# Decode attention with a GeGLU FFN on one core: longer weight rows in a ring of their own, and attention with the small operands stationary

## The chip, the core and the metric

The kernel runs on one core of a Trainium2 chip. Times are device microseconds (us) of that core; a profiled execution also gives a span, which is about 2 us shorter than the time. Engines: PE (TensorE, with PEld for its weight loads), DVE (VectorE), ACT (ScalarE), POOL (GpSimd), SP (which here only issues DMAs). A matmul loads a *stationary* operand and streams a *moving* one past it; I call one weight load plus one matmul a pair. The granted clock is the share of PE's full clock that the clock records of the profile show; landing records are the times at which each of the 16 DMA engines reports its part of a load as landed. Executions have a fast and a slow state; only fast runs are compared.

## The reference, cut to what matters

```python
xn = layernorm(x)                                   # 8 tokens, D = 512
q  = xn @ wq                                        # 32 heads of 128, 8 KV heads
k, v = last 1024 positions of the caches            # 8 batches x 8 KV heads x 1024 x 128, bf16
s  = (softmax(q @ k.T * Dh**-0.5) @ v) @ wo
g  = silu((gelu(xn @ w_gate) * (xn @ w_up)) @ w_down)   # F = 1792
return x + s * g
```

All of it is read once: 33.6 MB of K and V and 13.9 MB of weights, 47.46 MB by the profile.

## The kernel before

K, V and all weights pass through one ring of 21 slots of 8 KB per partition, in this order: K of group 0, wq, then K and V of 16 groups (4 batches of one KV head each), gate, up, down, wo. The compute loop runs over blocks of 1024 keys: transpose 8 K chunks on PE, copy them to SBUF, use each K^T chunk as the stationary operand for 16 columns of q, take exponentials at the end of a group, and use each V chunk as the stationary operand for 16 columns of P. V runs LAG = 6 blocks behind.

```python
ring = ...tile_pool(name="ring", bufs=21)
s_ps = ps_s.tile([P, P], FP32, name="s_ps")          # accumulator of the output product
nc.vector.memset(s_ps, 0.0)                           # cleared at the start
def score_block(n):
    for c in range(CB):
        nc.tensor.matmul(sc[g][:, s*CB + c, :], kT[n][:, c*P:(c+1)*P], qT_all[:, hkv, b0:b0+I, :], ...)
    if s == NB - 1:                                   # last block of a group: exponentials, ACT
        ...
def value_block(g, s):
    for c in range(s*CB, (s+1)*CB):
        nc.tensor.matmul(oT[g], v_t[g][:, c*Dh:(c+1)*Dh], pT[g][:, c, :], ...)
    if s == NB - 1:                                   # oT[g] is final: times 1/sum, DVE
        ...
# ... after the loop
expand_out(NM - 1); ffn_up(); select_out(NM - 1); ffn_down()
for m in range(NM):                                   # NM = 4 tiles of wo, 32 pairs each
    project_out(m)
# out = x + s_ps * g
```

The softmax here doesn't subtract the row's maximum and nothing guards it: scores larger than these inputs give would overflow.

## Time and profile before

| | before |
|---|---|
| time, median | 123.18 us (123.16 to 123.19) |
| span of the profiled execution | 121.1 us |
| PE / DVE / ACT busy | 71% / 60% / 19% |
| data read from HBM | 47.46 MB, 421 to 428 GB/s in every stage of 10 us from 5 to 105 us |

These lines are from the page of the kernel before: the span, busy time by engine, then slices of a fortieth of the span (DMA is the busy share of the 16 DMA engines in tenths), the main DMA queue, and the chain of work that ended last.

```profile
span 121.1 us, 4123 instructions
...
PE 86.0 (71%) x1856; PEld 71.1 (59%) x1856; DVE 72.3 (60%) x150; ACT 22.6 (19%) x70; POOL 2.4 (2%) x15
...
DMA  3999999999999999999999999999999999999820
GB/s 84 387 430 430 430 427 417 419 430 425 425 427 427 425 414 422 430 419 430 425 427 422 422 417 430 422 425 422 425 433 418 422 414 434 416 430 423 341 88 5
...
q1 hardware_dynamic: 6800, 47.46, 93.7%
...
DMA 82%; PE 12%; DVE 2%; SPq 1%; issue 0%
```

The DMA engines are full from the second slice to the thirty-seventh, and 82% of the chain is DMA: in the body the kernel is as fast as its loads. The next lines are from the timeline of the kernel before (start, duration, engine, line, operation, count, and in brackets the idle time ahead of the first instruction and what ended it).

```profile
93.11 0.61 PE L282 MATMUL kT_ps<-ident,slot 128*128 128x128 bf16 x8
...
95.28 1.14 ACT L304 ACTIVATE pT<-sc_ps,diag 128x128 bf16<-128x128 f32 x4 [2.39 <-PE sc_ps L294]
...
96.85 1.05 PE L329 MATMUL m_ps<-pT,slot 128*128 128x16 bf16 x32
...
98.70 7.69 PE L402 MATMUL m_ps<-slot,xpT_sb 128*32 128x512 bf16 x32
...
108.52 1.12 PE L437 MATMUL m_ps<-slot,hT_sb 128*8 128x128 bf16 x56 [0.55 <-DVE m_ps L433]
...
109.96 1.02 PE L383 MATMUL s_ps<-slot,oE_1066 128*8 128x128 bf16 x32 [0.32 <-DMA slot<-in_A_wo_dram]
...
112.40 1.02 PE L383 MATMUL s_ps<-slot,oE_1569 128*8 128x128 bf16 x32 [1.42 <-DMA slot<-in_A_wo_dram]
...
114.84 1.02 PE L383 MATMUL s_ps<-slot,oE_2072 128*8 128x128 bf16 x32 [1.42 <-DMA slot<-in_A_wo_dram]
...
116.75 1.02 PE L383 MATMUL s_ps<-slot,oE_2360 128*8 128x128 bf16 x32 [0.88 <-DMA slot<-in_A_wo_dram]
```

The four tiles of the output product each wait for their weights, and the kernel ends 1.02 us of PE work (plus two DVE steps and the store) after the last large piece lands.

### The profile page before, as it was taken

How to read it: one execution, taken by the hardware profiler on the slowest of the kernel's cores; microseconds unless marked ns; L12 is line 12 of the kernel's file. 1: busy time of each engine (PE TensorE's matmuls, PEld its weight loads, DVE VectorE, ACT ScalarE, POOL GpSimd, SP SyncE). 2: the span in 40 equal slices, each digit the busy share in tenths (PEclk: the TensorE clock that was granted, in tenths of full speed). 3: DMA queues.
4: the chain of work that ended last, by engine and by line, in shares of the span. 5: the costliest groups of instructions: out<-in, count | busy, mean ns of one | idle time of the engine just before them, and what ended most of it. 6: DMA issues, size and time to landing. Idle time of an engine off the chain costs nothing.

```text
span 121.1 us, 4123 instructions
## 1 busy us (share of the span) xinstructions
PE 86.0 (71%) x1856; PEld 71.1 (59%) x1856; DVE 72.3 (60%) x150; ACT 22.6 (19%) x70; POOL 2.4 (2%) x15
## 2 busy tenths in 40 slices
PE   0075269696875968999997969566798789955450
PEld 0061029586865957999896969565698542134340
DVE  2352046866956749678989987747798670562000
ACT  0440000321303301212330330303033300300000
POOL 6100000000000000000000000000000000000000
PEclk9999756999999985559999999999999756995555
DMA  3999999999999999999999999999999999999820
GB/s 84 387 430 430 430 427 417 419 430 425 425 427 427 425 414 422 430 419 430 425 427 422 422 417 430 422 425 422 425 433 418 422 414 434 416 430 423 341 88 5
DMA packets 6929, 47.73 MB, mean 394 GB/s; under 512 B 888, under 2 KB 896, under 8 KB 1920
## 3 DMA queue, kind: packets, MB, share of 16 engines
q1 hardware_dynamic: 6800, 47.46, 93.7%
q8 instruction: 14, 0.23, 0.7%
q10 hardware_dynamic: 112, 0.02, 0.1%
q14 instruction: 3, 0.02, 0.1%
HBM read 47.46 MB, written 0.01 MB: 392 GB/s over the span
## 4 chain that ended last, share of the span: by engine, by line
DMA 82%; PE 12%; DVE 2%; SPq 1%; issue 0%
DMA slot<-in_A_k_cache_dram 44%; DMA slot<-in_B_w_gate_dram 16%; DMA slot<-in_A_wo_dram 15%; DMA slot<-in_A_wq_dram 7%; PE kT_ps L282 7%; PE m_ps L329 2%; PE sc_ps L294 2%; SPq L91 1%; PE s_ps L383 1%; DVE kT L286 1%; PE m_ps L316 1%; DVE sums L318 1%; SPq L103 0%; PE m_ps L370 0%; DVE tmp L483 0%
## 5 line engine op out<-in xcount | busy, mean ns | idle before, releaser
L286 DVE COPY kT<-kT_ps 128x1024 bf16<-128x1024 bf16 x64 | 42.2, 677 | 18.1 <-PE kT_ps L282 17.5
L282 PE MATMUL kT_ps<-ident,slot 128*128 128x128 bf16 x512 | 43.4, 234 | 9.9 <-DMA slot<-in_A_k_cache_dram 9.5
L282 PEld LDWEIGHTS <-slot 128*128 128x128 bf16 x512 | 32.6, 104 | 13.3 <-DMA slot<-in_A_k_cache_dram 10.1
L304 ACT ACTIVATE pT<-sc_ps,diag 128x128 bf16<-128x128 f32 x64 | 18.2, 368 | 70.6 <-PE sc_ps L294 70.6
L294 PE MATMUL sc_ps<-qT_all,kT 128*128 128x16 bf16 x512 | 22.9, 171 | 0.3 <-issue 0.3
L329 PE MATMUL m_ps<-pT,slot 128*128 128x16 bf16 x512 | 21.8, 170 | 1.2 <-issue 1.1
L329 PEld LDWEIGHTS <-slot 128*128 128x128 bf16 x512 | 18.6, 97 | 4.6 <-issue 3.1
L294 PEld LDWEIGHTS <-kT 128*128 128x128 bf16 x512 | 20.4, 99 | 0.0
L318 DVE TENSOR_REDUCE sums<-m_ps 128x16 f32<-128x512 f32 x16 | 10.9, 684 | 1.2 <-PE m_ps L316 1.2
L402 PE MATMUL m_ps<-slot,xpT_sb 128*32 128x512 bf16 x32 | 7.7, 1105 | 0.0
L316 PE MATMUL m_ps<-pT,ones_pp 128*128 128x512 bf16 x16 | 6.7, 416 | 0.7 <-ACT pT L304 0.7
L250 PE MATMUL m_ps<-slot,xnT_sb 128*32 128x512 bf16 x32 | 3.5, 527 | 4.2 <-DMA slot<-in_A_wq_dram 4.2
L234 PE MATMUL m_ps<-ident,xhat 8*128 8x8 bf16 x4 | 0.3, 168 | 7.0 <-DVE xhat L214 7.0
L259 DVE CAST q_sb<-m_ps 128x512 bf16<-128x512 f32 x2 | 1.3, 686 | 6.6 <-PE m_ps L250 6.6
L356 DVE TENSOR_TENSOR wide<-m_ps,hmask 64x1024 bf16<-64x1024 bf16 x4 | 4.9, 1216 | 0.5 <-PE m_ps L352 0.4
L483 DVE TENSOR_TENSOR tmp<-s_ps,g_sb 128x128 f32<-128x128 f32 x1 | 0.3, 292 | 7.1 <-PE s_ps L383 7.1
L250 PEld LDWEIGHTS <-xnT_sb 128*32 128x32 bf16 x32 | 0.8, 101 | 6.2 <-issue 5.8
L322 DVE RECIPROCAL recip<-sums 128x16 f32<-128x16 f32 x16 | 4.0, 253 | 0.6
L234 PEld LDWEIGHTS <-xhat 8*128 8x128 bf16 x4 | 0.2, 102 | 7.0 <-DVE xhat L214 7.0
L402 PEld LDWEIGHTS <-xpT_sb 128*32 128x32 bf16 x32 | 1.7, 117 | 4.3 <-issue 3.4
L338 DVE TENSOR_TENSOR oT_all<-m_ps,recip 128x16 bf16<-128x16 f32 x16 | 3.5, 218 | 0.4 <-PE m_ps L329 0.3
L352 PE MATMUL m_ps<-ident,oT_all 128*64 128x128 bf16 x4 | 1.0, 253 | 2.7 <-DVE sums L318 2.1
(71 smaller groups left out, 33.4 us busy)
## 6 DMA issues: line engine op xcount, KB each, us to landing
slot<-in_A_k_cache_dram SPq DMA_DIRECT2D x16, 1024.0 KB, 19.4
slot<-in_A_v_cache_dram SPq DMA_DIRECT2D x16, 1024.0 KB, 19.7
slot<-in_A_wq_dram SPq DMA_DIRECT2D x4, 1024.0 KB, 8.6
slot<-in_A_wo_dram SPq DMA_DIRECT2D x3, 1024.0 KB, 18.0
slot<-in_B_w_gate_dram SPq DMA_DIRECT2D x2, 896.0 KB, 20.0
slot<-in_B_w_up_dram SPq DMA_DIRECT2D x2, 896.0 KB, 18.9
slot<-in_B_w_down_dram SPq DMA_DIRECT2D x2, 896.0 KB
slot<-in_A_wo_dram SPq DMA_DIRECT2D x1, 768.0 KB, 17.7
```

What stands on the lines that cost most here:

```text
L250: nc.tensor.matmul(q_ps[n][Q * q : Q * (q + 1), :], xnT_sb[:, k, :], wq_t[k][:, hkv * NW : (hkv + 1) * NW], start=(k == 0), stop=(k == NDC ...
L282: nc.tensor.transpose(t_ps[:, c * P : (c + 1) * P], k_t[g][:, cc * Dh : (cc + 1) * Dh], ident)
L286: nc.vector.tensor_copy(out=kT[n], in_=t_ps)
L294: nc.tensor.matmul(sc[g][:, s * CB + c, :], kT[n][:, c * P : (c + 1) * P], qT_all[:, hkv, b0 : b0 + I, :], start=True, stop=True,)
L304: nc.scalar.activation(out=pT[g][:, :, i * rep : (i + 1) * rep], in_=sc[g][:, :, i * rep : (i + 1) * rep], func=ACT.Exp, bias=diag[:, i : ...
L316: nc.tensor.matmul(sums_ps, ones_pp, pT[g], start=True, stop=True)
L318: nc.vector.tensor_reduce(out=sums, in_=sums_ps.rearrange("p c m -> p m c"), axis=AX.X, op=ALU.add)
L322: nc.vector.reciprocal(out=recip[g], in_=sums)
L329: nc.tensor.matmul(oT[g], v_t[g][:, c * Dh : (c + 1) * Dh], pT[g][:, c, :], start=(c == 0), stop=(c == C - 1),)
L338: nc.vector.tensor_tensor(out=oT_all[:, hkv * rep : (hkv + 1) * rep, b0 : b0 + I].rearrange("p j i -> p i j"), in0=oT[g].rearrange("p (i j ...
L356: nc.vector.tensor_tensor(out=wide, in0=t_ps.rearrange("p (q e) -> p e q", e=HS) .unsqueeze(2) .to_broadcast([HS * B, HS, HS, DQ]), in1=hm ...
L402: nc.tensor.matmul(gu_ps[w][Q * q : Q * (q + 1), :], xpT_sb[:, k, :], cols[:, j0[q] : j0[q] + JQ, :], start=(k == 0), stop=(k == NDC - 1), ...
```

## The change

Its intent: fewer, longer DMA rows for the weights, and far fewer PE instructions in attention. (1) Weights go through a ring of 4 slots of 16 KB; the K/V ring shrinks to 11. (2) q becomes the stationary operand, padded with zeros to 32 columns so that two groups share a tile, and K^T is the moving one, in four column tiles. (3) Exponentials are taken for a head (two groups) at a time; DVE transposes P in 32x32 blocks. (4) P is the stationary operand for V, in four column tiles whose partial sums a closing fp32 product with a selection matrix adds up. (5) To find PSUM banks, the output accumulator moves into a pool of the loop and is cleared at its first use. Not shown in the cut below: 16 of the 64 copies of K^T move from DVE to ACT, and the smaller pools get fewer buffers.

```diff
-    ring = ctx.enter_context(tc.tile_pool(name="ring", bufs=21))
+    ring = ctx.enter_context(tc.tile_pool(name="ring", bufs=11))
+    wide_ring = ctx.enter_context(tc.tile_pool(name="wide_ring", bufs=4))
 ...
+    def score_half(g, a):
+        for kb in range(P // Q):
+            nc.tensor.matmul(sc[hkv][Q * kb : Q * (kb + 1), a],
+                qz[:, hkv, half].rearrange("p h m -> p (h m)"),
+                kT[2 * g + a][:, :, Q * kb : Q * (kb + 1)], ...)
+    def exp_head(hkv): ...                  # ACT, 4 x 256 columns
+    def turn_head(hkv): nc.vector.transpose(out=pT[hkv]..., in_=p_sb[hkv]...)
 ...
     def value_block(g, s):
+            nc.tensor.matmul(o_ps[g][Q * t : Q * (t + 1), :],
+                pT[hkv][:, half, 2 * y : 2 * y + 2, :].rearrange("p c m -> p (c m)"),
+                v_t[g][:, 2 * y * Dh : (2 * y + 2) * Dh], ...)
+            o_sb[g] = small.tile([P, 2, Dh], FP32, name="o_sb")
+            nc.scalar.copy(out=o_sb[g]..., in_=o_ps[g])
+    def close_group(g):
+        for c in range(2):
+            nc.tensor.matmul(fin, o_sb[g][:, c, :], pick[:, c, :], start=(c == 0), stop=(c == 1))
 ...
     def project_out(m):
+        if m == 0:
+            s_ps.append(ps_o.tile([P, P], FP32, name="o_ps"))
+            nc.vector.memset(s_ps[0], 0.0)
 ...
-    LA, LAG = 2, 6
+    LA, LAG = 2, 13
 ...
+    for part in range(2):
+        expand_out(NM - 1, part)
     ffn_up()
     select_out(NM - 1)
     ffn_down()
     ...
     for m in range(NM):                     # NM is now 2, 64 pairs each
         project_out(m)
```

More of the change, by code (lines that the diff above doesn't have):

```diff
@@ L53 @@
     SLOT = C * Dh
+    WSLOT = 2 * SLOT
     JF = F // P
@@ L62 @@
     front.tile([P, 96], FP32, name="front_pad")
-    ring = ctx.enter_context(tc.tile_pool(name="ring", bufs=21))
+    ring = ctx.enter_context(tc.tile_pool(name="ring", bufs=11))
+    wide_ring = ctx.enter_context(tc.tile_pool(name="wide_ring", bufs=4))
     consts = ctx.enter_context(tc.tile_pool(name="consts", bufs=1))
     persist = ctx.enter_context(tc.tile_pool(name="persist", bufs=1))
-    kT_pool = ctx.enter_context(tc.tile_pool(name="kT_pool", bufs=4))
-    p_pool = ctx.enter_context(tc.tile_pool(name="p_pool", bufs=3))
-    small = ctx.enter_context(tc.tile_pool(name="small", bufs=3))
+    kT_pool = ctx.enter_context(tc.tile_pool(name="kT_pool", bufs=3))
+    p_pool = ctx.enter_context(tc.tile_pool(name="p_pool", bufs=2))
+    small = ctx.enter_context(tc.tile_pool(name="small", bufs=2))
     ps_kT = ctx.enter_context(tc.tile_pool(name="ps_kT", bufs=3, space=bass.MemoryType.PSUM))
-    ps_sc = ctx.enter_context(tc.tile_pool(name="ps_sc", bufs=2, space=bass.MemoryType.PSUM))
-    ps_m = ctx.enter_context(tc.tile_pool(name="ps_m", bufs=2, space=bass.MemoryType.PSUM))
-    ps_s = ctx.enter_context(tc.tile_pool(name="ps_s", bufs=1, space=bass.MemoryType.PSUM))
+    ps_sc = ctx.enter_context(tc.tile_pool(name="ps_sc", bufs=1, space=bass.MemoryType.PSUM))
+    ps_o = ctx.enter_context(tc.tile_pool(name="ps_o", bufs=2, space=bass.MemoryType.PSUM))
+    ps_m = ctx.enter_context(tc.tile_pool(name="ps_m", bufs=1, space=bass.MemoryType.PSUM))
     ctx.enter_context(tc.manual_schedule())
@@ L82, in slot, with wide_slot @@
         return ring.tile([P, SLOT], BF16, name="slot")
+    def wide_slot():
+        return wide_ring.tile([P, WSLOT], BF16, name="wide_slot")
     k_t, v_t, wo_t = {}, {}, {}
-    wq_t, wg_t, wu_t, wd_t = [], [], [], []
+    wq_t, ffn_t = [], []
     def load_cache(src, g):
@@ L100, in load_wq @@
     def load_wq():
-        for k in range(NDC):
-            t = slot()
-            nc.sync.dma_start(out=t, in_=A_wq[k * P : (k + 1) * P, :])
-            wq_t.append(t)
-    def load_ffn():
-        for dst, src in ((wg_t, B_w_gate), (wu_t, B_w_up)):
-            for a in range(2):
-                t = slot()
-                nc.sync.dma_start(
-                    out=t[:, 0 : 2 * F],
-                    in_=src[a * 2 * P : (a + 1) * 2 * P, :].rearrange(
-                        "(p k) f -> p (k f)", k=2
-                    ),
-                )
-                dst.append(t[:, 0 : 2 * F].rearrange("p (k f) -> p k f", k=2))
-        JH = JF // 2
-        wd = B_w_down.rearrange("(p j) d -> p j d", j=JF)
-        for a in range(2):
-            t = slot()[:, 0 : JH * D].rearrange("p (j d) -> p j d", j=JH)
-            nc.sync.dma_start(out=t, in_=wd[:, a * JH : (a + 1) * JH, :])
-            wd_t.extend(t[:, j, :] for j in range(JH))
-    HS = SLOT // D
+        for a in range(2):
+            t = wide_slot()
+            src = A_wq[a * 2 * P : (a + 1) * 2 * P, :].rearrange("(p k) n -> p (k n)", k=2)
+            nc.sync.dma_start(out=t, in_=src)
+            t = t.rearrange("p (k n) -> p k n", k=2)
+            wq_t.extend(t[:, k, :] for k in range(2))
+    def load_ffn():
+        for src, k in ((B_w_gate, NDC), (B_w_up, NDC), (B_w_down, JF)):
+            n = src.shape[0] * src.shape[1] // P
+            t = wide_slot()[:, 0:n]
+            nc.sync.dma_start(out=t, in_=src.rearrange("(p k) f -> p (k f)", k=k))
+            ffn_t.append(t.rearrange("p (k f) -> p k f", k=k))
+    HS = WSLOT // D
     NM = Hq // HS
@@ L129, in load_wo @@
     def load_wo(m, cut=HS):
-        t = slot().rearrange("p (e d) -> p e d", e=HS)
+        t = wide_slot().rearrange("p (e d) -> p e d", e=HS)
         src = A_wo[m * HS * Dh : (m + 1) * HS * Dh, :].rearrange("(p e) d -> p e d", e=HS)
@@ L157 @@
     nc.vector.memset(eps_sb, 1e-5)
-    sel = consts.tile([P, R, I], FP32, name="sel")
+    sel = consts.tile([P, P // IR, I, rep], FP32, name="sel")
     nc.gpsimd.memset(sel, 0.0)
@@ L162 @@
         out=sel, in_=sel, compare_op=ALU.not_equal, fill=1.0, base=0,
-        pattern=[[-I, R], [-1, I]], channel_multiplier=1,
+        pattern=[[-IR, P // IR], [-rep, I], [-1, rep]], channel_multiplier=1,
     )
@@ L166 @@
     nc.vector.tensor_reduce(
-        out=diag, in_=sel.rearrange("p r i -> p i r"), axis=AX.X, op=ALU.add
+        out=diag, in_=sel.rearrange("p k i j -> p i k j"), axis=AX.XY, op=ALU.add
     )
@@ L171 @@
     )
+    pick = consts.tile([P, 2, IR], FP32, name="pick")
+    nc.gpsimd.memset(pick, 0.0)
+    for t in range(P // Q):
+        nc.gpsimd.affine_select(
+            out=pick, in_=pick, compare_op=ALU.not_equal, fill=1.0, base=-Q * t,
+            pattern=[[-IR, 2], [-1, IR]], channel_multiplier=1,
+        )
     hmask = consts.tile([HS * B, HS], BF16, name="hmask")
@@ L222 @@
     nc.gpsimd.memset(xpT_sb, 0.0)
-    qT_all = persist.tile([P, Hkv, B, rep], BF16, name="qT_all")
+    qz = persist.tile([P, Hkv, GPH, GPH, IR], BF16, name="qz")
+    nc.gpsimd.memset(qz, 0.0)
     oT_all = persist.tile([P, Hq, B], BF16, name="oT_all")
@@ L226 @@
     g_sb = persist.tile([P, P], FP32, name="g_sb")
-    s_ps = ps_s.tile([P, P], FP32, name="s_ps")
-    nc.vector.memset(s_ps, 0.0)
     def transpose_x():
         t = ps_m.tile([P, 2, NDC, B], BF16, name="m_ps")
+        xn = xhat.rearrange("b (a p k) -> b a k p", a=2, k=2)
+        xp = xhat.rearrange("b (p k) -> b k p", k=NDC)
         for k in range(NDC):
-            nc.tensor.transpose(t[:, 0, k, :], xhat[:, k * P : (k + 1) * P], ident[0:B, 0:B])
-        xp = xhat.rearrange("b (a p k) -> b a k p", a=2, k=2)
-        for a in range(2):
-            for k in range(2):
-                nc.tensor.transpose(t[:, 1, 2 * a + k, :], xp[:, a, k, :], ident[0:B, 0:B])
+            nc.tensor.transpose(t[:, 0, k, :], xn[:, k // 2, k % 2, :], ident[0:B, 0:B])
+        for k in range(NDC):
+            nc.tensor.transpose(t[:, 1, k, :], xp[:, k, :], ident[0:B, 0:B])
         nc.vector.tensor_copy(out=xnT_sb[:, :, 0:B], in_=t[:, 0])
@@ L245, in project_q @@
         q_sb = persist.tile([P, Hkv // NQ, NW], BF16, name="q_sb")
-        q_ps = [ps_m.tile([P, NW], FP32, name="m_ps") for n in range(Hkv // NQ)]
+        q_ps = [ps_o.tile([P, NW], FP32, name="o_ps") for n in range(Hkv // NQ)]
         for k in range(NDC):
@@ L268, in project_q @@
         for n in range(Hkv // NQ):
-            nc.vector.tensor_copy(
-                out=qT_all[:, n * NQ : (n + 1) * NQ],
-                in_=t_ps[:, n, :, :, 0:B].rearrange("p j q b -> p q b j"),
-            )
-    kT, sc, pT, oT = {}, {}, {}, {}
+            for a in range(GPH):
+                nc.vector.tensor_copy(
+                    out=qz[:, n * NQ : (n + 1) * NQ, a, a, :].rearrange(
+                        "p q (b j) -> p q b j", b=I
+                    ),
+                    in_=t_ps[:, n, :, :, a * I : (a + 1) * I].rearrange("p j q b -> p q b j"),
+                )
@@ L277, in transpose_block @@
+    kT, sc, pT, p_sb, o_ps, o_sb, recip = {}, {}, {}, {}, {}, {}, {}
     def transpose_block(n):
         g, s = n // NB, n % NB
-        t_ps = ps_kT.tile([P, CB * P], BF16, name="kT_ps")
+        t_ps = ps_kT.tile([P, CB, P], BF16, name="kT_ps")
         for c in range(CB):
             cc = s * CB + c
-            nc.tensor.transpose(
-                t_ps[:, c * P : (c + 1) * P], k_t[g][:, cc * Dh : (cc + 1) * Dh], ident
-            )
-        kT[n] = kT_pool.tile([P, CB * P], BF16, name="kT")
@@ L286, in transpose_block @@
-        nc.vector.tensor_copy(out=kT[n], in_=t_ps)
-    def score_block(n):
-        g, s = n // NB, n % NB
-        hkv, b0 = g // GPH, (g % GPH) * I
+            nc.tensor.transpose(t_ps[:, c, :], k_t[g][:, cc * Dh : (cc + 1) * Dh], ident)
+        if n % 2 == 0:
+            kT[n // 2] = kT_pool.tile([P, 2 * CB, P], BF16, name="kT")
+        dst = kT[n // 2][:, (n % 2) * CB : (n % 2 + 1) * CB, :]
+        if n % (2 * NB) in (3, 6):
+            nc.scalar.copy(out=dst, in_=t_ps)
+        else:
+            nc.vector.tensor_copy(out=dst, in_=t_ps)
@@ new lines, in score_half @@
+    def score_half(g, a):
+        hkv, half = g // GPH, g % GPH
+        if half == 0 and a == 0:
+            sc[hkv] = ps_sc.tile([P, 2, 2 * CB, Q], FP32, name="sc_ps")
+        for kb in range(P // Q):
+            nc.tensor.matmul(
+                sc[hkv][Q * kb : Q * (kb + 1), a],
+                qz[:, hkv, half].rearrange("p h m -> p (h m)"),
+                kT[2 * g + a][:, :, Q * kb : Q * (kb + 1)],
+                start=(half == 0),
+                stop=(half == GPH - 1),
+                skip_group_check=True,
+            )
@@ new lines, in exp_head, with turn_head @@
+    def exp_head(hkv):
+        p_sb[hkv] = p_pool.tile([P, C * Q], BF16, name="p_sb")
+        src = sc[hkv].rearrange("p a c (r i) -> p (a c r) i", i=I)
+        dst = p_sb[hkv].rearrange("p (n i) -> p n i", i=I)
+        for i in range(I):
+            nc.scalar.activation(
+                out=dst[:, :, i], in_=src[:, :, i], func=ACT.Exp,
+                bias=diag[:, i : i + 1], scale=inv_sqrt_dh,
+            )
+    def turn_head(hkv):
+        pT[hkv] = p_pool.tile([P, GPH, C, IR], BF16, name="pT")
+        nc.vector.transpose(
+            out=pT[hkv].rearrange("p h c m -> p c h m"),
+            in_=p_sb[hkv].rearrange("p (c h m) -> p c h m", c=C, h=GPH),
+        )
@@ new lines, in sum_head @@
+    def sum_head(hkv):
+        sums_ps = ps_m.tile([P, GPH, CB, IR], FP32, name="m_ps")
+        for s in range(NB):
+            nc.tensor.matmul(
+                sums_ps, ones_pp, pT[hkv][:, :, s * CB : (s + 1) * CB, :],
+                start=(s == 0), stop=(s == NB - 1),
+            )
+        sums = small.tile([P, GPH, IR], FP32, name="sums")
+        nc.vector.tensor_reduce(
+            out=sums, in_=sums_ps.rearrange("p h c m -> p h m c"), axis=AX.X, op=ALU.add
+        )
+        recip[hkv] = small.tile([P, GPH, IR], FP32, name="recip")
+        nc.vector.reciprocal(out=recip[hkv], in_=sums)
@@ L291, in score_block, with value_block @@
+    def value_block(g, s):
+        hkv, half = g // GPH, g % GPH
         if s == 0:
-            sc[g] = ps_sc.tile([P, C, IR], FP32, name="sc_ps")
-        for c in range(CB):
+            o_ps[g] = ps_o.tile([P, 2 * Dh], FP32, name="o_ps")
+        for y in range(s * CB // 2, (s + 1) * CB // 2):
+            t = y % (P // Q)
             nc.tensor.matmul(
-                sc[g][:, s * CB + c, :],
-                kT[n][:, c * P : (c + 1) * P],
-                qT_all[:, hkv, b0 : b0 + I, :],
-                start=True,
-                stop=True,
+                o_ps[g][Q * t : Q * (t + 1), :],
+                pT[hkv][:, half, 2 * y : 2 * y + 2, :].rearrange("p c m -> p (c m)"),
+                v_t[g][:, 2 * y * Dh : (2 * y + 2) * Dh],
+                start=(y < P // Q),
+                stop=(y >= C // 2 - P // Q),
+                skip_group_check=True,
@@ L300, in score_block @@
             )
         if s == NB - 1:
-            pT[g] = p_pool.tile([P, C, IR], BF16, name="pT")
-            for i in range(I):
-                nc.scalar.activation(
-                    out=pT[g][:, :, i * rep : (i + 1) * rep],
-                    in_=sc[g][:, :, i * rep : (i + 1) * rep],
-                    func=ACT.Exp,
-                    bias=diag[:, i : i + 1],
-                    scale=inv_sqrt_dh,
-                )
-    recip = {}
-    def sum_group(g):
-        sums_ps = ps_m.tile([P, C, IR], FP32, name="m_ps")
-        nc.tensor.matmul(sums_ps, ones_pp, pT[g], start=True, stop=True)
-        sums = small.tile([P, IR], FP32, name="sums")
-        nc.vector.tensor_reduce(
-            out=sums, in_=sums_ps.rearrange("p c m -> p m c"), axis=AX.X, op=ALU.add
-        )
-        recip[g] = small.tile([P, IR], FP32, name="recip")
-        nc.vector.reciprocal(out=recip[g], in_=sums)
@@ L324, in value_block @@
-    def value_block(g, s):
-        if s == 0:
-            sum_group(g)
-            oT[g] = ps_m.tile([P, IR], FP32, name="m_ps")
-        for c in range(s * CB, (s + 1) * CB):
-            nc.tensor.matmul(
-                oT[g],
-                v_t[g][:, c * Dh : (c + 1) * Dh],
-                pT[g][:, c, :],
-                start=(c == 0),
-                stop=(c == C - 1),
-            )
-        if s == NB - 1:
-            hkv, b0 = g // GPH, (g % GPH) * I
-            nc.vector.tensor_tensor(
-                out=oT_all[:, hkv * rep : (hkv + 1) * rep, b0 : b0 + I].rearrange(
-                    "p j i -> p i j"
-                ),
-                in0=oT[g].rearrange("p (i j) -> p i j", i=I),
-                in1=recip[g].rearrange("p (i j) -> p i j", i=I),
-                op=ALU.mult,
-            )
@@ L347 @@
-    oE, wide_t = {}, {}
-    def expand_out(m):
-        t_ps = ps_m.tile([HS * B, Dh], BF16, name="m_ps")
-        nc.tensor.transpose(
-            t_ps, oT_all[:, m * HS : (m + 1) * HS, :].rearrange("p h b -> p (h b)"), ident
-        )
-        wide = small.tile([HS * B, HS, HS, DQ], BF16, name="wide")
-        nc.vector.tensor_tensor(
-            out=wide,
-            in0=t_ps.rearrange("p (q e) -> p e q", e=HS)
-            .unsqueeze(2)
-            .to_broadcast([HS * B, HS, HS, DQ]),
-            in1=hmask.unsqueeze(1).unsqueeze(3).to_broadcast([HS * B, HS, HS, DQ]),
+            o_sb[g] = small.tile([P, 2, Dh], FP32, name="o_sb")
@@ new lines, in value_block @@
+            nc.scalar.copy(out=o_sb[g].rearrange("p c d -> p (c d)"), in_=o_ps[g])
+    def close_group(g):
+        hkv, half = g // GPH, g % GPH
+        fin = ps_m.tile([P, IR], FP32, name="m_ps")
+        for c in range(2):
+            nc.tensor.matmul(fin, o_sb[g][:, c, :], pick[:, c, :], start=(c == 0), stop=(c == 1))
+        nc.vector.tensor_tensor(
+            out=oT_all[:, hkv * rep : (hkv + 1) * rep, half * I : (half + 1) * I].rearrange(
+                "p j i -> p i j"
+            ),
+            in0=fin.rearrange("p (i j) -> p i j", i=I),
+            in1=recip[hkv][:, half, :].rearrange("p (i j) -> p i j", i=I),
@@ L362, in expand_out @@
             op=ALU.mult,
         )
-        wide_t[m] = wide
+    oE, wide_t, x_ps, s_ps = {}, {}, {}, []
+    def expand_out(m, part):
+        if part == 0:
+            x_ps[m] = ps_m.tile([HS * B, Dh], BF16, name="m_ps")
+            nc.tensor.transpose(
+                x_ps[m], oT_all[:, m * HS : (m + 1) * HS, :].rearrange("p h b -> p (h b)"), ident
+            )
+            wide_t[m] = small.tile([HS * B, HS, HS, DQ], BF16, name="wide", bufs=1)
+        HE = HS // 2
+        es = slice(part * HE, (part + 1) * HE)
+        nc.vector.tensor_tensor(
+            out=wide_t[m][:, es],
+            in0=x_ps[m].rearrange("p (q e) -> p e q", e=HS)[:, es]
+            .unsqueeze(2)
+            .to_broadcast([HS * B, HE, HS, DQ]),
+            in1=hmask.unsqueeze(1).unsqueeze(3).to_broadcast([HS * B, HE, HS, DQ]),
+            op=ALU.mult,
+        )
@@ L383, in project_out @@
                 nc.tensor.matmul(
-                    s_ps[32 * q : 32 * q + B, :],
+                    s_ps[0][32 * q : 32 * q + B, :],
                     oE[m][:, e, :],
@@ L396, in ffn_up @@
     def ffn_up():
-        gu_ps = [ps_m.tile([P, JQ * P], FP32, name="m_ps") for w in range(2)]
-        for w, wt in enumerate((wg_t, wu_t)):
+        gu_ps = [ps_o.tile([P, JQ * P], FP32, name="o_ps") for w in range(2)]
+        for w, wt in enumerate(ffn_t[0:2]):
             for k in range(NDC):
-                cols = wt[k // 2][:, k % 2, :].rearrange("x (p j) -> x j p", j=JF)
+                cols = wt[:, k, :].rearrange("x (p j) -> x j p", j=JF)
                 for q in range(NQ):
@@ L439, in ffn_down @@
                     hT_sb[:, j - j0[r], Q * r : Q * r + B],
-                    wd_t[j][:, q * P : (q + 1) * P],
+                    ffn_t[2][:, j, q * P : (q + 1) * P],
                     start=(j == 0),
@@ L450, in ffn_down @@
         nc.vector.tensor_tensor(out=g_sb, in0=th2, in1=f_ps, op=ALU.mult)
-    LA, LAG = 2, 6
+    LA, LAG = 2, 13
     N = NG * NB
+    NH = GPH * NB
     transpose_x()
-    for n in range(LA):
+    for n in range(NB):
         transpose_block(n)
     project_q()
-    for n in range(N + LAG):
-        if n + LA < N:
-            transpose_block(n + LA)
-        if n < N:
-            score_block(n)
-        if n >= LAG:
-            g, s = (n - LAG) // NB, (n - LAG) % NB
-            value_block(g, s)
-            GM = HS // rep * GPH
-            if g % GM == 0 and g > 0:
-                if s == 0:
-                    expand_out(g // GM - 1)
-                if s == 3:
-                    select_out(g // GM - 1)
-    expand_out(NM - 1)
+    for n in range(LA, N + LAG + NB):
+        if NB <= n < N:
+            transpose_block(n)
+        k = n - LA
+        if 0 <= k < N and k % 2 == 1:
+            score_half(k // NB, k % NB // 2)
+            if k % NH == NH - 1:
+                exp_head(k // NH)
+        if n >= NH and n % NH == 3 and n // NH <= Hkv:
+            turn_head(n // NH - 1)
+        if n >= NH and n % NH == 4 and n // NH <= Hkv:
+            sum_head(n // NH - 1)
+        v = n - LAG
+        if 0 <= v < N:
+            value_block(v // NB, v % NB)
+        if v >= NB and v % NB == 1:
+            g = v // NB - 1
+            close_group(g)
+        if v == N // 2 + 2:
+            expand_out(0, 0)
+        if v == N // 2 + 4:
+            expand_out(0, 1)
+        if v == N // 2 + 6:
+            select_out(0)
+    for part in range(2):
+        expand_out(NM - 1, part)
     ffn_up()
@@ L482 @@
     tmp = small.tile([P, P], FP32, name="tmp")
-    nc.vector.tensor_tensor(out=tmp, in0=s_ps, in1=g_sb, op=ALU.mult)
+    nc.vector.tensor_tensor(out=tmp, in0=s_ps[0], in1=g_sb, op=ALU.mult)
     out_sb = small.tile([P, P], BF16, name="out_sb")
```

## The prediction

> **What bounds it now.** The DMA stream. The table of stages shows 418 to 434 GB/s and full engines from 5 to 112 us; the queue table has 47.46 MB on one queue. In the chain of waits DMA is 82%, PE 12%. PE (71% busy), DVE (60%) and ACT (19%) wait: by the list of waits PE waits 9.5 us and its weight loads 10.1 us for K tiles.
>
> In the packet records rows of 8192 B take 309 ns, 7168 B 272 ns, 2048 B 84 ns: about 27.7 B/ns plus 12 to 13 ns per row.
>
> The engines do not finish together. By the landing records, the last load reaches them between 114.2 and 117.3 us. The lag grows in steps of about 1.4 us, each after one of the 14 16-KB instruction fetches (22.5 to 113.7 us). The first eight hit eight different engines; from the ninth (76.3 us) the same ones are hit again, so the last engine is 3.1 us behind. They follow PE's 3712 instructions, one per 256.
>
> Tail: the last 0.75 MB lands at 116.7 us, then 32 matmul and weight-load pairs of project_out take 1.02 us, then two DVE steps and the store, to 121.1 us.
>
> **What the change does.**
> 1. Weight rows: 1920 become 1024 (q 512→256, FFN 768→384, out 640→384). 896 × 12.5 ns / 16 engines = −0.7 us. The Trainium skill, "DMA: Bandwidth & Descriptors" (Why small descriptors are slow), says each packet has a fixed overhead; this trace agrees, with its 12 ns.
> 2. PE pairs fall from 1856 to about 1246 (scores 512→128, V 512→256, +32 closing): 2492 instructions, so 9 fetches instead of 14. With 8 the last engine would be hit once (−1.5 us). The ninth falls near instruction 2304, as project_out begins (111 to 113 us), and probably still delays an already hit engine. I expect −0.2 us at 70%, −1.5 us at 30%.
> 3. Tail: after the last tile's large piece lands, 64 pairs are left instead of 32: +1.0 us.
> 4. P turned on DVE, extra copies on ACT, fp32 closing matmuls: off the critical path (DVE near 65 us, ACT near 45 us).
> 5. The ring shrinks from 21 to 11 slots and V is consumed 13 blocks after K instead of 6. An estimate from traced durations (a block's transposes 0.46 us at full clock, 0.9 at half) leaves 10 us of slack before a V slot is needed again, less 2 to 3 us of PE lag: no DMA gap at full clock. At half clock for long, it would stall. The last output tile waits for the gate's slot, free at about 104 us, needed at about 109 us.
>
> Sum: −0.7 −0.5 +1.0, plus a small allowance for stalls;
>
> **Predicted: 122.8 us, 80% range 121.3 to 124.6. Faster by over 2%: 0.08; within 2%: 0.80; slower by over 2%: 0.12.**
>
> **What would show it.** Right: 16 KB rows near 605 ns; 420 GB/s or more in all loop stages; 9 instruction fetches; 64 pairs of about 2 us after the last large landing; PE well below 71% at nearly the same time. Wrong: stages under 410 GB/s with DMA issues waiting for PE (ring too small) or for the gate's matmuls.
>
> **What would make it wrong.** A clock that stays at half, since more of PE is transposes: PE lags over 7 us and the ring starves (125 us or more). Only eight effective fetches, or a cheaper tail: 121.5 us or less.

## The result, and the profile after

The changed kernel takes **127.49 us** (127.23 to 127.53), against 123.18 us. The ratio is 1.0346 with a 95% interval of 1.0328 to 1.0364. (A ratio is the mean time of one kernel's fast runs over that of the other's of the same rounds, so not quite the ratio of the medians quoted.) The prediction, 122.8 us with a range to 124.6, was wrong.

The same page lines after the change:

```profile
span 125.8 us, 3010 instructions
...
PE 94.7 (75%) x1294; PEld 60.8 (48%) x1294; DVE 66.5 (53%) x126; ACT 45.8 (36%) x70; POOL 4.1 (3%) x21
...
DMA  3999999999999999999999999999999999988000
GB/s 86 417 449 423 404 427 435 417 425 427 435 419 422 427 430 417 425 427 425 422 435 414 427 425 425 427 425 422 444 436 425 433 421 438 354 292 344 0 5 3
...
q1 hardware_dynamic: 5792, 47.45, 90.2%
...
PE 38%; DMA 36%; DVE 11%; ACT 8%; issue 3%; SPq 1%; DVEq 0%; ACTq 0%
```

Up to slice 34 (107 us) the DMA rows look like those of before: the loop did not starve. Then the rate dips (354, 292, 344) and the last three slices, over 9 us, move nothing, where before only the last slices were thin. The chain has turned over: DMA went from 82% to 36%, and PE, DVE and ACT together from 14% to 57%. So the loads are not what the end waits for. The timeline of the changed kernel shows what is, from the last K transposes on:

```profile
92.16 0.61 PE L290 MATMUL kT_ps<-ident,slot 128*128 128x128 bf16 x8
...
94.01 2.53 ACT L320 ACTIVATE p_sb<-sc_ps,diag 128x256 bf16<-128x256 f32 x4 [0.21 <-PE sc_ps L306]
...
96.56 1.25 DVE L327 STREAM_TRANSPOSE pT<-p_sb 128x1024 bf16<-128x1024 bf16 x1 [1.58 <-ACT p_sb L320]
...
97.87 0.61 PE L335 MATMUL m_ps<-pT,ones_pp 128*128 128x256 bf16 x4 [2.92 <-DVE pT L327]
...
99.34 1.04 PE L369 MATMUL m_ps<-pick,o_sb 128*128 128x16 f32 x4
...
101.45 1.03 PE L369 MATMUL m_ps<-pick,o_sb 128*128 128x16 f32 x4
...
103.57 1.03 PE L369 MATMUL m_ps<-pick,o_sb 128*128 128x16 f32 x4 [0.53 <-ACT o_sb L363]
...
105.14 7.47 PE L439 MATMUL o_ps<-wide_slot,xpT_sb 128*32 128x512 bf16 x32
...
115.67 1.66 PE L474 MATMUL m_ps<-wide_slot,hT_sb 128*8 128x128 bf16 x56 [0.65 <-DVE m_ps L470]
...
118.48 0.17 DVE L417 MEMSET o_ps<- 128x128 f32 x1
118.70 3.59 PE L420 MATMUL o_ps<-wide_slot,oE 128*8 128x128 bf16 x128 [1.36 <-DVE o_ps L417]
```

Read it against the timeline before. The last K block is transposed 0.95 us *earlier* (92.77 against 93.72 us), but the FFN's first product starts at 105.14 instead of 98.70 us. Between them everything runs in series: exponentials of a whole head, the turn on DVE, sums, V, and three closings of about a microsecond each, with an ACT copy ahead of each. Then the output product starts only after the accumulator is cleared at 118.48 us, which DVE does behind the gate's last step, and all 128 pairs are still to do when they start at 118.70 us, 1.9 us after the last weights have landed (116.8 us by the landing records).

The account in microseconds closes:

| | before | after | difference |
|---|---|---|---|
| last K block transposed to FFN start (the drain) | 4.98 | 12.37 | +7.39 |
| last K block transposed, when | 93.72 | 92.77 | -0.95 |
| FFN start until output pairs could start, without DMA waits | 10.95 | 13.56 | +2.61 |
| all output pairs | 4.08 | 3.59 | -0.49 |
| sum of these | | | +8.56 |
| slack that before had | | | -4.04 |
| **end of the output product, 117.77 to 122.29** | | | **+4.52** |

The change's chain is 8.6 us longer; the first 4 us vanished in the slack; the rest is the 4.3 us of the result (4.5 in these two profiled executions).

Two more views. First, engine busy time and clock by stage; the columns are the stage, its length, busy us (instructions) of PE, PEld, DVE, ACT and POOL, then PE's granted clock, the DMA share and GB/s. After the change:

```profile
85.00:95.00 10.00, 8.73 (x128) 5.62 (x120) 5.97 (x11) 6.13 (x10) 0.00 (x0) 1.00 1.02 432
95.00:105.00 10.00, 6.07 (x53) 4.06 (x53) 2.71 (x6) 2.65 (x6) 0.00 (x0) 0.67 1.02 432
105.00:115.00 10.00, 8.53 (x53) 1.66 (x53) 5.70 (x8) 1.23 (x2) 0.00 (x0) 0.82 0.91 358
```

PE stood idle for 2.92 us waiting for the turn (to 97.87 us), and by the clock records the granted clock fell from 1.00 to 0.50 at 98.45 us: in the rest of the drain PE works at half speed. (The kernel before loses clock here too, at 95.51 us, although PE was idle for no longer than 0.40 us at a stretch in the 3.4 us ahead of it, so the length of an idle stretch alone does not explain when the clock falls. But its drain is 5 us long, not 12.) Second, the waits of the DMA queue's own sequencer, after the change (who waited for whom, total us, times, longest):

```profile
SPq L96 <- PE kT_ps L290: 28.3, 17, 2.3
SPq L132 <- DMA wide_slot<-in_B_w_gate_dram: 13.9, 1, 13.9
...
SPq L132 <- PE o_ps L439: 11.5, 1, 11.5
```

The small ring does make loads wait for PE (28.3 us in total), but with loads queued 18 us ahead this opened no gap. The last line is a real gap: the second half of wo needs the gate's slot, which is free only when the late FFN has read it, at 109.0 us. That is the dip in the GB/s row, and it is a rival explanation of the loss.

### The profile page after: what moved, and what is told of

It is laid out like the page before. It is cut to its first block, busy times and chain, and to the rows that moved or that the text cites. A ratio compares the mean times of both kernels' runs of the same rounds, so it can differ in the third digit from the quotient of the medians.

```text
span 125.8 us, 3010 instructions
## 1 busy us (share of the span) xinstructions
PE 94.7 (75%) x1294; PEld 60.8 (48%) x1294; DVE 66.5 (53%) x126; ACT 45.8 (36%) x70; POOL 4.1 (3%) x21
## 4 chain that ended last, share of the span: by engine, by line
PE 38%; DMA 36%; DVE 11%; ACT 8%; issue 3%; SPq 1%; DVEq 0%; ACTq 0%
DMA slot<-in_A_k_cache_dram 29%; PE kT_ps L290 13%; DMA wide_slot<-in_A_wq_dram 7%; ACT p_sb L320 6%; PE m_ps L369 5%; PE o_ps L353 5%; PE sc_ps L306 4%; DVE pT L327 4%; PE o_ps L439 3%; PE o_ps L420 3%; PE m_ps L335 3%; SPq L96 1%; PE m_ps L474 1%; DVE kT L297 1%; DVE wide L391 1%
## 5 line engine op out<-in xcount | busy, mean ns | idle before, releaser
L290 PEld LDWEIGHTS <-slot 128*128 128x128 bf16 x512 | 33.7, 107 | 12.8 <-issue 5.8
L297 DVE COPY kT<-kT_ps 128x1024 bf16<-128x1024 bf16 x48 | 32.9, 688 | 12.4 <-PE kT_ps L290 12.3
L295 ACT COPY kT<-kT_ps 128x1024 bf16<-128x1024 bf16 x16 | 16.7, 1046 | 25.2 <-PE kT_ps L290 21.4
L320 ACT ACTIVATE p_sb<-sc_ps,diag 128x256 bf16<-128x256 f32 x32 | 20.3, 826 | 3.7 <-PE sc_ps L306 3.7
L353 PE MATMUL o_ps<-slot,pT 128*32 128x256 bf16 x256 | 18.3, 300 | 0.0
L306 PE MATMUL sc_ps<-kT,qz 128*32 128x512 bf16 x128 | 13.4, 409 | 6.0 <-ACT p_sb L320 5.4
L327 DVE STREAM_TRANSPOSE pT<-p_sb 128x1024 bf16<-128x1024 bf16 x8 | 10.0, 1244 | 7.5 <-ACT p_sb L320 7.5
L369 PE MATMUL m_ps<-pick,o_sb 128*128 128x16 f32 x64 | 11.1, 288 | 1.9 <-DVE wide L391 1.1
L369 PEld LDWEIGHTS m_ps<-pick,o_sb 128*128 128x128 f32 x64 | 9.6, 214 | 5.0 <-ACT o_sb L363 2.2
L439 PE MATMUL o_ps<-wide_slot,xpT_sb 128*32 128x512 bf16 x32 | 7.5, 1090 | 0.0
```

Of the source, the lines that this page charges most:

```text
L290: nc.tensor.transpose(t_ps[:, c, :], k_t[g][:, cc * Dh : (cc + 1) * Dh], ident)
L295: nc.scalar.copy(out=dst, in_=t_ps)
L297: nc.vector.tensor_copy(out=dst, in_=t_ps)
L306: nc.tensor.matmul(sc[hkv][Q * kb : Q * (kb + 1), a], qz[:, hkv, half].rearrange("p h m -> p (h m)"), kT[2 * g + a][:, :, Q * kb : Q * (kb ...
L320: nc.scalar.activation(out=dst[:, :, i], in_=src[:, :, i], func=ACT.Exp, bias=diag[:, i : i + 1], scale=inv_sqrt_dh,)
L327: nc.vector.transpose(out=pT[hkv].rearrange("p h c m -> p c h m"), in_=p_sb[hkv].rearrange("p (c h m) -> p c h m", c=C, h=GPH),)
```

## The experiments

Theory T: the loss is the serial tail (drain, FFN, late clearing, all 128 pairs). Rival R1: the load that waits for the gate's slot. Rival R2: the small ring or the long rows. All kernels gave correct results. "Before" on the chips of these runs was 123.14 to 123.15 us; the changed kernel was not run again beside them, so gains are against its 127.49 us.

### Halves of the change: `x4_weights_only`, `x5_attention_only`

```diff
  # x4: before.py with load_wq, load_ffn, load_wo, ring 11 + wide ring 4 of the change; attention of before
  # x5: the change with load_wq, load_ffn, load_wo of before, one ring of 20 slots; attention of the change
```

> The attention of before with the long weight rows, their ring of 4 and the small ring of 11 slots. Theory T: -0.7 us for 896 fewer rows, +1.0 us for 64 pairs instead of 32 after the last large piece, perhaps 0.5 us for the wait for the gate's buffer: 123.0 to 124.2 us. Rival R2 (ring or rows are the loss): 126 us or more.

> The new attention with the weight slots of before (20 slots of 8 KB rows, no wide ring). Theory T: the drain stays, FFN starts near 105 us and the 128 output pairs start near 118.5 us, with all weights already landed: 126.5 to 127.7 us. Rival R2: near 123.2 us. Rival R1: near 123.2 us as well, since no load waits for the gate.

Weights only: 123.51 us (123.43 to 123.63), ratio 1.0028 [1.0010, 1.0046]. Attention only: 126.59 us (126.20 to 127.25), ratio 1.0284 [1.0242, 1.0325]. Each as T expected. R2 falls: with the small ring and the long rows the time is +0.4 us. R1 falls as the main cause: in the second kernel no load waits for the gate's matmuls, all weights have landed by 115.7 us, and the end is as late. These are its FFN and output product:

```profile
105.43 7.47 PE L446 MATMUL o_ps<-slot,xpT_sb 128*32 128x512 bf16 x32
...
118.30 3.59 PE L427 MATMUL o_ps<-slot,oE 128*8 128x128 bf16 x128 [1.36 <-DVE o_ps L424]
```

The first kernel ends as the kernel before does, with a wait for its last weights:

```profile
116.42 1.88 PE L380 MATMUL s_ps<-wide_slot,oE 128*8 128x128 bf16 x64 [2.36 <-DMA wide_slot<-in_A_wo_dram]
```

### The wait for the gate's slot alone: `x2_gate_own`

```diff
+        for a in range(2):                       # gate into two slots of the K/V ring
+            t = slot()[:, 0 : 2 * F].rearrange("p (k f) -> p k f", k=2)
+            nc.sync.dma_start(out=t, in_=B_w_gate.rearrange("(p k) f -> p k f", k=NDC)[:, 2*a : 2*a + 2, :])
-        for src, k in ((B_w_gate, NDC), (B_w_up, NDC), (B_w_down, JF)):
+        for src, k in ((B_w_up, NDC), (B_w_down, JF)):
```

> The gate weights go into two of the small slots, so the last output load no longer waits for the gate's matmuls. Theory T: the DMA gap at 110 to 115 us closes and the last load lands near 115 us, but the output pairs still start at about 118.7 us, so 127.2 to 127.7 us, no change. Rival R1: the time falls by 2 to 4 us.

Two of its four runs were slow (up to 129.03 us), which makes the median 128.19; the two fast ones are 126.84 and 127.49 us, ratio 1.0325 [1.0287, 1.0362]. (The slow two are slow by their time; their granted clocks, 0.906 and 0.891, are not lower than those of the fast two, and why they are slow stays open.) The gap closed (last load landed at 115.4 instead of 116.8 us) and the output pairs still waited for the clearing:

```profile
117.95 3.59 PE L428 MATMUL o_ps<-wide_slot,oE 128*8 128x128 bf16 x128 [1.36 <-DVE o_ps L425]
```

A DMA gap in full view of the GB/s row cost nothing that the two fast runs show (0.65 us apart), because something else was later.

### The accumulator: `x1_acc_early`

```diff
     def project_out(m):
-        if m == 0:
-            s_ps.append(ps_o.tile([P, P], FP32, name="o_ps"))
-            nc.vector.memset(s_ps[0], 0.0)
 ...
+        if n == N + 1:                            # in a bank that the K transposes have left
+            s_ps.append(ps_kT.tile([P, P], FP32, name="kT_ps"))
+            nc.vector.memset(s_ps[0], 0.0)
```

> Theory T (the loss is the serial drain: last exponentials, turn, values, fp32 closing, then FFN, then all 128 output pairs): the output pairs waited 1.36 us for the accumulator's clearing, which VectorE does only after the gate; with the accumulator cleared before the tail the pairs start right behind the down projection, so 126.1 us (-1.2 to -1.4 against the changed kernel's 127.5). Rival R1 (the last output load waits for the gate's buffer, and that load is the limit): it lands at about 116.5 us in any case, so less than 0.5 us is gained. Rival R2 (small ring or weight rows): no change.

125.24 us (125.07 to 126.35), ratio 1.0187 [1.0141, 1.0234]: 2.2 us gained, more than the wait itself. Its trace says why:

```profile
115.87 1.67 PE L471 MATMUL m_ps<-wide_slot,hT_sb 128*8 128x128 bf16 x56 [0.65 <-DVE m_ps L467]
...
117.32 2.58 PE L417 MATMUL kT_ps<-wide_slot,oE 128*8 128x128 bf16 x128
```

The pairs now follow the down projection without a pause, and they take 2.58 us instead of 3.59: the granted clock was back at 1.00 from 118.6 us, where the changed kernel still had 0.50. That the missing pause of 1.36 us brought this raise is argued, not shown: in y1b (next section) the clock rose at 118.95 us, with the same pause still there. The run at 126.35 us perhaps missed that raise; it was not profiled.

### The closing product: `y1_close_bf16`, `y1b_close_bf16`

```diff
-    pick = consts.tile([P, 2, IR], FP32, name="pick")
+    pick = consts.tile([P, 2, IR], BF16, name="pick")
-            o_sb[g] = small.tile([P, 2, Dh], FP32, name="o_sb")
+            o_sb[g] = small.tile([P, 2, Dh], BF16, name="o_sb")
```

> The closing product in bf16 instead of fp32 (32 pairs instead of 64, each cheaper). Theory T: the three closings behind the last K tile took 1.04, 1.03 and 1.03 us at half clock and lie in the serial drain, so FFN starts 1.5 to 2 us earlier (103.2 instead of 105.1 us) and the time is 125.5 to 126.2 us. A rival in which the end is set by DMA or by FFN's own weights gives no change from 127.5.

> The bf16 closing once more, because its profile fell into a slow execution and its fast runs gained 3.1 us where I had expected 1.5 to 2. If the gain is real it comes again (124.0 to 124.8 us), and its trace shows where: FFN should start at 102 to 103 us instead of 105.1, the rest a clock that is back at full speed in the tail or K tiles finished earlier in the loop.

The three fast executions of the first run took 123.71 to 124.43 us, ratio 1.0082 [1.0052, 1.0111] (its median, 124.37 us, includes a slow one); the second run took 124.32 us (124.29 to 124.66), ratio 1.0094 [1.0077, 1.0111]: two lines return 3.2 of the 4.3 us. I had expected 1.5 to 2. The last closing and the FFN in the second run's trace:

```profile
101.63 0.22 PE L369 MATMUL m_ps<-pick,o_sb 128*128 128x16 bf16 x2 [0.54 <-ACT o_sb L363]
...
102.40 7.56 PE L439 MATMUL o_ps<-wide_slot,xpT_sb 128*32 128x512 bf16 x32
```

A closing fell from 1.03 to 0.22 us at the same low clock, and it is 2 pairs instead of 4. FFN starts 2.74 us earlier: 2.0 us from the three closings, 0.75 us because the loop, where 13 more of them stand, is shorter too. Most of the rest is the output pairs (3.35 instead of 3.59 us).

One execution of the first run took 144.88 us (slow, not compared), and the profile fell on it. Eight K transposes took 0.94 to 1.07 us in it, instead of 0.61 us. The kernel before takes 1.01 to 1.04 us for them where its clock is 0.52 (45 to 55 us), so PE ran at about half speed in this execution, though its page has no clock row at all (the table of stages prints 1.00 where there are no records). The reason for that state stays open. The DMA rate fell to 277 GB/s in the loop, and the queue waited 26.2 us for the gate's slot. This is the failure that the prediction named under "what would make it wrong"; it is not what the ordinary runs do.

### The clock in the drain: `y4_keep_warm`

```diff
+        if n == N + 4:                            # while PE waits for the last turn
+            t = ps_kT.tile([P, 4, P], FP32, name="kT_ps")
+            for _ in range(13):
+                nc.tensor.matmul(t, ones_pp, kT[N // 2 - 1][:, 0:4, :], start=True, stop=True)
```

> The changed kernel plus 13 dummy products of 512 columns on PE in the 3 us in which it waits for the last head's exponentials and turn (result unchanged). If the fallen clock (0.5 from about 97.8 us) is a part of the drain's cost, the drain from the turn to FFN shrinks from 7.3 us to 5 to 6 us and the time falls by 1 to 2.5 us; if the drain is latency of the hops between engines alone, it stays within 0.5 us of 127.5.

125.41 us (124.92 to 126.39), ratio 1.0191 [1.0133, 1.0249]: 2.1 us gained by useless work. Stages of this run (columns as above):

```profile
95.00:98.00 3.00, 2.84 (x16) 1.19 (x13) 1.41 (x2) 1.75 (x4) 0.00 (x0) 1.00 0.96 402
98.00:101.00 3.00, 2.34 (x38) 1.46 (x37) 1.03 (x4) 0.75 (x2) 0.00 (x0) 1.00 1.02 435
```

The second of these stages in the changed kernel:

```profile
98.00:101.00 3.00, 2.90 (x36) 1.87 (x34) 1.01 (x3) 0.37 (x1) 0.00 (x0) 0.57 0.97 416
```

And a closing, from the timeline of y4 again:

```profile
100.93 0.62 PE L369 MATMUL m_ps<-pick,o_sb 128*128 128x16 f32 x4 [0.32 <-ACT o_sb L363]
```

The clock stays at 1.00 through the drain (it falls at 104.19 us, in the FFN), where the changed kernel had 0.57 from 98 to 101 us, and an fp32 closing takes 0.62 us. So about 1.6 us of the drain (FFN at 103.52 instead of 105.14 us) is the fallen clock. The gains of this section overlap: a cheaper closing is worth less when the clock is up.

### Both small edits: `u1_bf16_acc_early`

The edits are those of y1b and x1 together, on the changed kernel.

> Bf16 closing and early accumulator together, everything else as changed. Both shorten the same serial tail, so they add: the accumulator's 1.4 us of waiting on top of 124.4, 122.6 to 123.6 us; if the clock's part of both gains is the same microsecond, 123.5 or above. If they did not lie on the same chain, the smaller one would vanish.

123.40 us (123.33 to 123.57), ratio 1.0023 [1.0008, 1.0038]. Two small edits, none in the stream or the loop's structure, return 4.1 of the 4.3 us. Alone they returned 2.2 and 3.2; the sum is smaller, since the clock's part of x1's gain is missing here: in u1's trace the output pairs take 3.9 us (114.17 to 118.06 us, with a pause of 0.42 us that the profile puts to no wait) instead of 2.58:

```profile
114.17 3.01 PE L417 MATMUL kT_ps<-wide_slot,oE 128*8 128x128 bf16 x109
...
117.61 0.45 PE L417 MATMUL kT_ps<-wide_slot,oE 128*8 128x128 bf16 x19 [0.42 <-issue]
```

### A tail in another order: `y2_ffn_first`, `y3_ffn_first_plus`, `z1_reordered_tail`

Gate and up wait for weights that land at 97 and 101 us, just when PE stands idle for the last head. So: emit their products, and the gelu chain, ahead of the last head's sums and V, in PSUM banks that the K transposes have left; emit the first 64 output pairs ahead of the second half's selection.

```diff
# y2
-        gu_ps = [ps_o.tile([P, JQ * P], FP32, name="o_ps") for w in range(2)]
+        gu_ps = [ps_kT.tile([P, JQ * P], FP32, name="kT_ps") for w in range(2)]
+        if n == N + 4:
+            hidden = ffn_up()                     # ahead of sum_head of the last head
 ...     # turn_hidden(hidden) behind it; accumulator early as in x1
     ffn_down()
+    project_out(0)
     select_out(NM - 1)
+    project_out(1)
# y3 = y2 + bf16 closing + last wo tile in three pieces (8, 6, 2 blocks) instead of two (14, 2)
# z1 = y3, and
-        f_ps = ps_m.tile([P, P], FP32, name="m_ps")
+        f_ps = ps_sc.tile([P, P], FP32, name="sc_ps")
+        if n == N + 7:
+            ffn_down()                            # among the last V blocks
```

> Gate and up products and the gelu chain moved ahead of the last head's drain (into PSUM banks that the K transposes have left), accumulator cleared early, the first half of the output product ahead of the second half's selection. Theory T: PE meets the gate weights at about 97 us, the drain hides behind the gelu chain, the wait for the gate's buffer costs nothing because it is free at about 100 us, and the end is again the last landing (115 to 116 us) plus 64 pairs: 122.0 to 123.6 us. If the loss were in the stream or in the loop, the time would stay above 125 us.

> As the run before, with bf16 closing and with the last output tile loaded in three pieces (8, 6 and 2 blocks), so that 32 pairs are left after the last large landing, as in the kernel of before. 121.2 to 122.6 us, about 1 us under the run before it; this may beat both kernels.

> The reordered tail with the down projection moved ahead of the last head's expansion (its accumulator in a bank that the scores have left), so that PE no longer waits 2.7 us for VectorE's expansion. The last landing (about 115 us for the large piece) plus 32 pairs becomes the end: 121.2 to 122.6 us. If it does not fall under 123.2, the stream is not what is left.

The first two missed: 125.54 us (125.08 to 125.90), ratio 1.0193 [1.0161, 1.0225], and 123.80 us (123.61 to 123.95), ratio 1.0052 [1.0037, 1.0067]. By the letter of its expectation y2, above 125 us, would have spoken for the stream or the loop; its trace shows another cause. The FFN did start at 97.4 us, but I had left the down projection behind the last head's expansion. This is it in the first of them:

```profile
111.78 2.35 DVE L391 TENSOR_TENSOR wide<-m_ps,hmask 128x1024 bf16<-128x1024 bf16 x2 [0.32 <-PE m_ps L385]
...
114.45 1.67 PE L474 MATMUL m_ps<-wide_slot,hT_sb 128*8 128x128 bf16 x56 [2.71 <-DVE m_ps L470]
```

Its accumulator's clearing stood behind 2.35 us of expansion in DVE's order, PE idled 2.71 us, and the clock fell again. The third moves it: **122.66 us** (122.64 to 122.81), ratio **0.9963 [0.9948, 0.9978]**, 0.5 us faster than the kernel before (and 0.06 us above the range I had expected). Its end is like the one of before, the last large landing plus 32 pairs:

```profile
115.00 1.02 PE L418 MATMUL kT_ps<-wide_slot,oE 128*8 128x128 bf16 x32 [0.39 <-DVE oE L413]
116.48 1.02 PE L418 MATMUL kT_ps<-wide_slot,oE 128*8 128x128 bf16 x32 [0.46 <-DMA wide_slot<-in_A_wo_dram]
```

## Why the prediction was wrong, point by point

**The step that failed is the fourth**: "P turned on DVE, extra copies on ACT, fp32 closing matmuls: off the critical path". It holds in the loop, where engines wait for K tiles. It is false behind the last K tile, where nothing is left to hide behind: there the drain grew from 4.98 to 12.37 us. The busy times that this step gave were right (DVE 66.5 us, ACT 45.8 us); what was wrong is the path. The prediction never took an account of the tail with its slack of 4.0 us. The closings alone, which it sent off the critical path, were worth 3.2 us (y1b). What the exponentials of a whole head and the turn on DVE cost was not tested alone: with the two small edits of u1 the drain is still 10.4 us (92.13 to 102.50 us), and nearly all of the loss is gone.

**Third step, the tail, "64 pairs are left instead of 32: +1.0 us"**: right where the rest is on time (in x4 the last 64 pairs take 1.88 us instead of 1.02), but in the changed kernel 128 pairs were left, 3.59 us, because they waited for DVE's clearing of the accumulator and not for a landing. The prediction read the diff's move of the clearing past the gate without asking what stands ahead of it in DVE's order.

**First step, rows, -0.7 us**: right in kind, too large. A 16 KB row takes 611 ns, not the 605 I expected from a fixed 12 to 13 ns per row, and a 14 KB row 535 ns against 2 x 272. That is 0.45 us over all weights by these durations (0.11 for wq, 0.22 for the FFN, 0.12 for wo, each over 16 engines). The landing records of x4 show the least delayed engine 0.4 us earlier at the end of wo's first half (108.85 us, against 109.22).

**Second step, instruction fetches**: the mechanism agrees with the traces, the pair count was low. PE has 1294 pairs, not 1246: each fp32 product became two pairs, and the sums use 32 pairs where they had 16. PE's busy share did not end "well below 71%" either, as the prediction had it: it is 75% (94.7 us, with 11.1 us of fp32 closings). There were 10 fetches, the first eight by 95.5 us and the ninth at 116.4 us, after the loads. The landing records (us behind the first of the 16 engines, for one late load) show the effect:

```
before, 13 fetches ahead of it (of 14):     0.00 0.02 0.03 0.06 0.24 0.35 0.58 0.87 1.44 1.48 1.63 2.84 2.91 2.93 3.10 3.11
after,  8 fetches ahead of it:              0.00 0.01 0.04 0.05 0.19 0.39 0.71 0.95 1.45 1.46 1.61 1.62 1.67 1.69 1.70 1.70
```

The last engine was 1.7 us late instead of 3.1, as forecast for eight fetches. The changed kernel could not use this, since its end no longer waited for loads. In z1 it counted: there the ninth fetch comes at 113.2 us, and the large piece that lands next is complete on fifteen engines at 114.97 us and on the last one at 116.44 us (3.1 us from first to last, where the piece ahead of it took 1.7). PE waited 0.46 us for it. (No run changed the number of fetches alone, so the cause is read from coincidence in time, in every trace, and not from an experiment.)

**Fifth step, the ring**: no gap in the loop, as predicted (423 GB/s or more in every stage of 10 us from 5 to 105 us). The gate's slot, "free at about 104 us", was free at 109.0, because the FFN was late; x2 shows that this cost nothing.

**The clock** was named as a risk for the loop; it struck in the drain instead, for about 1.6 us there (y4) and up to 1.0 us in the output pairs (x1).

On what the argument drew from the Trainium skill: "DMA: Bandwidth & Descriptors", section "Why small descriptors are slow", says that each packet carries a fixed overhead; the rows above agree, at 7 to 9 ns saved for each row merged into another. "TensorE: Matmul & The Clock Gate", section "Why this matters for your kernels", advises against PE-idle gaps over about 3 us between matmul bursts; here the clock fell to 0.50 just after a gap of 2.92 us, and with the gap filled (y4) it stayed at 1.00 through the drain. But in the kernel before it fell at 95.51 us with no gap over 0.40 us in the 3.4 us ahead, so such gaps are not its only cause. The same page, Part 3, says that products with at most 32 stationary columns run concurrently in column tiles; the trace agrees, as four products of 512 columns took 0.40 us together, and the scores' PE time fell from 22.9 to 13.4 us, which bought nothing. "FP8 and Floating Point Precision", section "TensorE Precision Notes", says that true fp32 takes 4 passes; this trace shows two pairs per product, with weight loads of 192 ns where bf16 has 98.

## What to carry to other kernels

In a kernel bound by its loads, judge a change by two separate sums: the stream, and the serial chain that follows the last tile each stage needs, with the slack that this chain has before the last landing. A change that works on larger groups (a head instead of a group, LAG 13 instead of 6) and adds hops between engines lengthens that second chain even if it needs far fewer instructions, and in this drain PE also lost its clock after standing idle. When a tail is late, look first at the order of emission: a clearing behind a long DVE step, a product behind a wait, a precision that the result does not need.

## What the Trainium skill lacked or had wrong

- "DMA: Bandwidth & Descriptors" has no time for long rows of an HBM load on the SP queue: here 84 ns for 2 KB, 272 for 7 KB, 309 for 8 KB, 535 for 14 KB, 611 for 16 KB per DMA engine.
- Neither "Runtime: NRT & Kernel Launch" (instruction fetch) nor "DMA: Bandwidth & Descriptors" (queues) has a figure for what an instruction fetch costs the data on its DMA engine: here 16 KB per 256 PE instructions, 0.88 to 1.03 us each in the two kernels, and the landing records fit one engine that is about 1.4 us further behind after each, with eight engines hit in turn (eight engines late after 8 fetches, five of them twice as late after 13).
- "TensorE: Matmul & The Clock Gate" gives an idle window of about 3.4 us as what brings the clock down (and 3 us as advice). Gaps of that length were not needed here: the clock fell at 44.31 and 95.51 us in the kernel before and at 104.19 us in y4, with no PE gap over 1.09, 0.40 and 0.53 us in the 3.4 us ahead of each. What does decide it, these runs do not show. Its warning that clock records can be unreliable fits the 144.88 us execution, which ran at about half speed by its durations (0.94 to 1.07 us for eight transposes instead of 0.61) and left no clock records.
- "FP8 and Floating Point Precision" speaks of 4 passes for fp32 but not of instructions: one fp32 product is two pairs here, and a closing of two products with 16 moving columns took 1.03 us against 0.22 in bf16, both at half clock.
